# Attention scores from stacked high and low key parts: whole-array matmuls in place of 64-row pairs, in a top-k attention and gated feed-forward kernel

## The chip, the cores and the metric

The kernel runs on one core of one Trainium2 chip. The time is device microseconds of one execution; three runs were taken.

## What is computed

Inputs are q, k and v of 4 batches, 8 heads, 576 positions and 64 dimensions, two feed-forward weights of 512 x 1536 and one of 1536 x 512, and a norm weight. The weights come as 64-bit floats.

```
scores = (q @ k.T) / 8                      # per batch and head, 576 x 576
kth    = 32nd largest of each row
attn   = softmax(where(scores >= kth, scores, -1e9))
x      = (attn @ v), heads side by side     # 2304 x 512
xn     = x / sqrt(mean(x*x) + 1e-6) * rms_g
g      = xn @ w_gate
out    = (g * sigmoid(g) * (xn @ w_val)) @ w_out
```

The scores need more than one reduced-precision pass, since the 32nd largest must be found exactly enough. Each operand is split in a high part (a copy into the reduced type F32R) and a low part (what the copy lost), and the products of the parts are summed in PSUM.

## The kernel before

**Steps and jobs.** The work is cut into 72 steps. An ordinary step is one block of 128 queries for one pair of heads (e = 0 and 1); a tail step takes the last 64 queries of two pairs. A batch has 16 ordinary and 2 tail steps. Two ordinary steps, or one tail step, make a job, which has its own query preparation (`prep_q` and its like, through `turned`). A step makes scores for 576 keys in two halves of 288 for each head, so four PSUM banks: two halves times two heads.

**A step's chain.** `attend` adds the score matmuls (TensorE, PE), four copies of a bank to the SBUF tile `sp` (ScalarE, ACT), then `topk` (VectorE, DVE): elementwise minimum and maximum of the two halves (`mn`, `mx`), then rounds of eight maxima (MAX8) and their removal (MATCH_REPLACE8). Then come the threshold `bt` (GpSimd, POOL), a mask `rr` (ACT), its subtraction (POOL), the exponential with its row sums (ACT), nine transposes of `sp` (PE, L575), their copies, and the value products (PE, `pt`/`ptt` with `vt`).

**Feed-forward.** Ten units of 128 or 256 tokens (`feed_forward`). Each does rows of gate and value matmuls (`wgh`, `wgl`, `wvh`, `wvl` with `xth`, `xtl`; called gate matmuls below, 256 columns) and of output matmuls (`wo`, 512 columns). The gate weights stay in SBUF. The output weights pass through two buffers `wo`, 512 KB a load; the first unit makes them and stores them in `wosc`, later units load them from there. The weights' 64-bit halves are turned to 32-bit floats in 36 pieces of 128 x 512: two VectorE operations each (L357, L358), one of ACT, two of POOL, and again one of ACT for the high part. A raw piece comes into `xvt`, `tg` or later `kraw`.

**Row tiling in the scores.** A head has 64 dimensions, so the two heads of a pair lie on rows 0 to 63 and 64 to 127 of the tiles `kh`, `kl` (keys, high and low) and `qh`, `ql`. For each half there are three products, qh kh, ql kh and qh kl, for each head: twelve matmuls of 64 rows and 288 columns in an ordinary step, alternating between the heads.

**What sets the order.** All operations are recorded in a plan with a priority (`pri`, the step's number plus offsets from the table `PR`), a duration and the keys that they read and write. `place` lays them out engine by engine; `emit` writes every engine's instructions in the order of the starts that `place` finds. Each engine then runs its own list in order. SP's list holds all DMAs, so a DMA that waits there holds back those behind it. Score, transpose, gate and other short-lived results share six banks; two are kept for the output sums.

The program has a second, exact version behind a flag that is not set with these inputs; it is not executed.

Of the kernel before, what the change touches and what calls it, by code (L numbers as in the profile page):

```python
# [9 lines left out]
F32 = mybir.dt.float32  # L10
F32R = mybir.dt.float32r
U32 = mybir.dt.uint32
# [12 lines left out]
    HV=7, SU=1, ZU=6, F1=5.02, FX0=-3.08, FS0=0.39, FD0=-2.4, Z0=0, QN=0, FE=-9.01, EV=-2.13, SO=-2.7, WP1=0.21, WI=-6.69, FO=2.17, FS=0.8, ZP=0, KO=-4.26, WP0=1.0, FB=3.5, AO=0.79, FX=-16.28, QO=-3, TB=0.35, WO=-1.76, SM=1.12,  # L25
# [13 lines left out]
SWITCH = 0.2  # L39

# [191 lines left out]
def tile_topk_attention_moe(  # L232
# [25 lines left out]
    def sb(name, shape, dt=F32):  # L258
        return cp.tile(list(shape), dt, name=name, tag=name)
# [3 lines left out]
    NS, NK, NV, NQ, NPT, NWO, NQR = 5, 4, 2, 3, 4, 2, 2  # L263
# [5 lines left out]
    kh = [sb(f"kh{i}", [128, S + 64], F32R) for i in range(NK)]  # L269
    kl = [sb(f"kl{i}", [128, S + 64], F32R) for i in range(NK)]  # L270
# [3 lines left out]
    qh = [sb(f"qh{i}", [128, 2, 128], F32R) for i in range(NQ)]  # L274
    ql = [sb(f"ql{i}", [128, 2, 128], F32R) for i in range(NQ)]
# [38 lines left out]
    def build(exact):  # L314
# [22 lines left out]
        def weight_piece(src, half, hi, lo, keyh, keyl, pri):  # L337
# [9 lines left out]
            else:  # L347
# [51 lines left out]

        def prep_k(b, pair, pri):  # L400

# [5 lines left out]
            ko = pri + PR["KO"]  # L407
            if g == 0:
# [17 lines left out]
            add(PE, 0.44, tr, r=(("kraw", g, 0), ("kraw", g, 1)), w=(("kh", s, 0), ("kl", s, 0), ("pt", z)), bank=bank, pri=ko)  # L426
            split(bank, z, 512, kh[s][:, 64:576], kl[s][:, 64:576], ("kh", s, 0), ("kl", s, 0), ko)
# [17 lines left out]
        def turned(raw, rkeys, pri):  # L445
# [8 lines left out]
            add(PE, 0.218, tr, r=rkeys, w=(("qh", s), ("ql", s), ("pt", y)), bank=bank, pri=pri + PR["QO"])  # L454
            hi, lo = (t[s].rearrange("p z t -> p (z t)") for t in (qh, ql))
            split(bank, y, 256, hi, lo, ("qh", s), ("ql", s), pri + PR["QO"])
# [35 lines left out]
        def topk(i, e, bank, pri):  # L492
# [18 lines left out]
            add(DVE, 0.372, lambda: nc.vector.tensor_tensor(mn[:, e, :], bank.tile[:, 0:half], b, op=ALU.min), r=bk, w=(nk,), bank=bank, pri=pri)  # L511
            add(DVE, 0.37, lambda: nc.vector.tensor_tensor(row[:, 0:half], bank.tile[:, 0:half], b, op=ALU.max), r=bk + (("turn", 0),), w=(mk,), bank=bank, pri=pri)
# [380 lines left out]
```

## Time and profile before

| | |
|---|---|
| median of 3 runs | 878.14 us (877.94 to 878.2) |
| profiled execution, its own time | 879.04 us |
| its span, first to last instruction | 876.8 us |
| TensorE busy | 798.7 us, 91% |
| VectorE busy | 726.7 us, 83% |
| ScalarE busy | 617.6 us, 70% |
| GpSimd busy | 488.1 us, 56% |
| mean granted TensorE clock | 0.95 |

The profiled execution takes 2.2 us more than its span. Busy time is a share of the whole span; stages differ. PE's rows give each matmul from its start to its modelled end, and matmuls overlap, so the distance between the starts of two rows says what one costs. A line number of a helper (L321) stands for many matmuls; the tile names tell them apart.

### The profile page before, as it was taken

Reading aid. Unit: us, or ns where it says so; the run is one execution under the profiler, and the core shown is the slowest. Engines: PE = TensorE matmul, PEld = TensorE weight load, DVE = VectorE, ACT = ScalarE, POOL = GpSimd, SP = SyncE. Lnnn points to the kernel's source line nnn. Section 1 sums busy time; section 2 is a strip of 40 time slices with the busy share of each in tenths; the row PEclk is TensorE's granted clock in tenths of the full one; section 3 lists DMA queues with packets and bytes.
Section 4 is the critical chain, followed back from the end, with each engine's and each line's share of the span. In section 5 each row is a group of like instructions: output and inputs, shape, how many; then the busy total and the mean of one; then the engine's idle time right before and its main releaser. Section 6 shows DMA issues by size and latency. Waiting matters only on the chain.

```text
span 876.8 us, 19543 instructions
## 1 busy us (share of the span) xinstructions
PE 798.7 (91%) x6770; PEld 701.6 (80%) x6770; DVE 726.7 (83%) x2292; ACT 617.6 (70%) x1529; POOL 488.1 (56%) x690
## 2 busy tenths in 40 slices
PE   5656766899799999999999999999999999999996
PEld 3545745788598888989988888999889988889995
DVE  5999989999889999999899999659998469993211
ACT  6777775898687888778777887666786557874221
POOL 5778989866644564457553644665654244444121
PEclk9978766799799999999999999999999999999998
DMA  7443676455633333244343332333532252232353
GB/s 209 127 117 117 225 224 219 151 172 156 198 96 93 100 108 102 90 111 142 101 145 101 118 120 93 107 121 110 179 93 67 83 174 85 91 127 95 112 164 107
DMA packets 86653, 112.92 MB, mean 129 GB/s; under 512 B 50832, under 2 KB 64144, under 8 KB 86544
## 3 DMA queue, kind: packets, MB, share of 16 engines
q1 hardware_dynamic: 86544, 111.57, 40.8%
q8 instruction: 55, 0.90, 0.4%
q14 instruction: 54, 0.44, 0.2%
HBM read 100.53 MB, written 11.01 MB: 127 GB/s over the span
## 4 chain that ended last, share of the span: by engine, by line
PE 77%; DVE 10%; DMA 6%; ACT 3%; POOL 2%; issue 1%; SPq 0%; DVEq 0%; ACTq 0%; POOLq 0%
PE bank L321 66%; PE bank L575 8%; DVE mx L516 2%; DVE mx L518 2%; DMA wo<-wosc 2%; DMA xvt<-in_moe_w_gate_dram 2%; PE bank L425 1%; DVE bank L357 1%; PE bank L453 1%; DMA kraw<-in_k_dram 1%; DMA xvt<-in_moe_w_out_dram 1%; DVE mx L513 1%; ACT sp L552 1%; PE bank L672 1%; PE bank L637 1%
## 5 line engine op out<-in xcount | busy, mean ns | idle before, releaser
L516 DVE MAX8 mx<-mx 128x8 f32<-128x296 f32 x576 | 242.4, 455 | 0.0
L551 POOL TENSOR_TENSOR sp<-sp,rr 128x576 f32<-128x576 f32 x144 | 184.2, 1290 | 44.7 <-ACT rr L550 42.8
L518 DVE MATCH_REPLACE8 mx<-mx 128x296 f32<-128x296 f32 x432 | 192.2, 451 | 0.0
L321 PE MATMUL bank<-wo,hh 128*128 128x512 f32 x432 | 149.4, 426 | 11.8 <-DMA wo<-wosc 8.4
L740 POOL TENSOR_TENSOR hl<-tg,hh 128x256 fp32r<-128x256 f32 x108 | 79.5, 737 | 115.8 <-ACT hh L739 105.7
L575 PE MATMUL bank<-ident,sp 128*128 128x128 f32 x648 | 100.1, 286 | 29.1 <-ACT sp L552 25.5
L552 ACT ACTIVATE sp<-sp,bt 128x576 f32<-128x576 f32 x144 | 113.1, 787 | 13.7 <-POOL sp L551 13.0
L550 ACT ACTIVATE rr<-sp,bt 128x576 bf16<-128x576 f32 x144 | 108.5, 779 | 17.7 <-POOL bt L546 17.4
L539 ACT COPY sp<-bank 128x288 f32<-128x288 f32 x288 | 97.1, 409 | 24.2 <-PE bank L321 23.4
L321 PE MATMUL bank<-xth,wgh 128*128 128x256 f32 x384 | 113.5, 296 | 0.2 <-ACT xv L593 0.2
L575 PEld LDWEIGHTS bank<-ident,sp 128*128 128x128 f32 x648 | 77.6, 146 | 43.8 <-ACT sp L552 30.6
L321 PE MATMUL bank<-xth,wvh 128*128 128x256 f32 x384 | 110.5, 288 | 0.0
L321 PE MATMUL bank<-xth,wgl 128*128 128x256 f32 x384 | 107.2, 279 | 0.0
L321 PE MATMUL bank<-xtl,wgh 128*128 128x256 f32 x384 | 107.2, 279 | 0.0
L321 PE MATMUL bank<-xth,wvl 128*128 128x256 f32 x384 | 107.2, 279 | 0.0
L321 PE MATMUL bank<-xtl,wvh 128*128 128x256 f32 x384 | 107.2, 279 | 0.0
L727 DVE SCALAR_TENSOR_TENSOR tg<-tg,bank 128x256 f32<-128x256 f32 x108 | 44.3, 411 | 68.5 <-ACT tg L721 68.3
L577 ACT COPY pt<-bank 128x512 f32<-128x512 f32 x144 | 83.1, 595 | 13.1 <-PE bank L575 12.6
L321 PEld LDWEIGHTS bank<-wo,hh 128*128 128x128 f32 x432 | 71.9, 194 | 25.0 <-DMA wo<-wosc 8.3
L721 ACT ACTIVATE tg<-bank 128x256 f32<-128x256 f32 x108 | 41.3, 383 | 69.0 <-PE bank L321 55.1
L321 PE MATMUL bank<-wo,hl 128*128 128x512 f32 x216 | 86.6, 401 | 0.0
L546 POOL TENSOR_TENSOR bt<-mx,cst 128x6 f32<-128x6 f32 x72 | 14.4, 200 | 125.3 <-DVE mx L516 124.3
(147 smaller groups left out, 2052.6 us busy)
## 6 DMA issues: line engine op xcount, KB each, us to landing
wo<-wosc SPq DMA_DIRECT2D x108, 512.0 KB, 3.4
vt<-in_v_dram SPq DMA_DIRECT2D x52, 256.0 KB, 3.0
xvt<-in_moe_w_gate_dram SPq DMA_DIRECT2D x12, 512.0 KB, 4.5
wosc<-wo SPq DMA_DIRECT2D x12, 512.0 KB, 3.2
kraw<-in_k_dram SPq DMA_DIRECT2D x32, 128.0 KB, 3.1
kraw<-in_moe_w_val_dram SPq DMA_DIRECT2D x8, 512.0 KB, 4.1
qraw<-in_q_dram SPq DMA_DIRECT2D x56, 64.0 KB, 2.8
out_dram<-osb SPq DMA_DIRECT2D x14, 256.0 KB, 2.3
```

What stands on the lines that cost most here:

```text
L321: nc.tensor.matmul(o, l, r, start=start, stop=stop)
L516: add(DVE, 0.381, lambda o8=o8: nc.vector.max(o8, row[:, 0:half + 8]), w=(mk,), pri=pri + 0.1 * n)
L518: add(DVE, 0.436, lambda o8=o8: nc.vector.match_replace(row[:, 0:half + 8], o8, row[:, 0:half + 8], NEG), w=(mk,), pri=pri + 0.1 * n)
L539: add(ACT, 0.32, lambda b=bank[half, e], c0=c0: nc.scalar.copy(sp[s][:, c0:c0 + 288], b.tile[:, 0:288]), w=(("sp", s, e, half),), bank=ban ...
L550: add(ACT, 0.7, lambda e=e, tl=tl: nc.scalar.activation(rr[e], tl, AF.Relu, bias=bt[t][:, e, 2:3], scale=-BIG), r=(("bt", t),) + spkeys(i, ...
L551: add(POOL, 1.27, lambda e=e, tl=tl: nc.gpsimd.tensor_tensor(tl, tl, rr[e], op=ALU.subtract), r=(("rr", e),), w=spkeys(i, e), pri=pri + PR ...
L552: add(ACT, 0.8, lambda e=e, tl=tl: nc.scalar.activation(tl, tl, AF.Exp, bias=bt[t][:, e, 1:2], scale=SCALE, accum_out=sums(e)[0]), r=(("bt ...
L575: nc.tensor.transpose(bank.tile[:, c * 128:(c + 1) * 128], sp[s][:, c0 + c * 128:c0 + (c + 1) * 128], ident)
L577: add(ACT, 0.228 if n == 1 else 0.507, lambda dst=dst, bank=bank, n=n: nc.scalar.copy(dst[:, 0:n * 128], bank.tile[:, 0:n * 128]), w=(key, ...
L721: add(ACT, 0.325, lambda gb=gb, hs=hs: nc.scalar.activation(th[hs], gb.tile[:, 0:256], AF.Tanh, scale=1.0 if halves[0] else 0.5), w=(("th" ...
L727: add(DVE, 0.365, lambda gb=gb, hs=hs: nc.vector.scalar_tensor_tensor(th[hs], th[hs], 1.0, gb.tile[:, 0:256], op0=ALU.add, op1=ALU.mult), ...
L740: add(POOL, 0.75, lambda hs=hs: nc.gpsimd.tensor_tensor(hl[hs], th[hs], hh[hs].bitcast(F32), op=ALU.subtract), r=(("th", hs), ("hh", hs)), ...
```

## The change

Scores become matmuls over all 128 rows. For each pair there are now two key tiles, `kt[s][0]` and `kt[s][1]`, one for each head: one half of the rows holds the head's high part, the other half its low part. The query tiles `qh` and `ql` are twice as wide: for each head they hold the high (or low) part of that head's queries on both halves of the rows. One matmul of `qh` with `kt` gives qh kh + qh kl, one of `ql` gives ql kh + ql kl, so a half for one head takes two matmuls in place of three, and the product of the two low parts is now included.

[...] The query's high copy is 512 columns wide instead of 256; its low part is subtracted into `pt`.

`attend` adds four score operations a step, each with one bank and two matmuls (four in a tail step), where one operation held all four banks. The table of offsets is replaced as a whole; some offsets have a second part that counts for the first 14 steps (`early`, `E0`). `ZP` goes from 0 to 1: in the units from the seventh on, a third of the gate activations go through ACT and POOL instead of VectorE. Three other branches are added that these values leave unused (`WS` = 0, `PM` = 72, `XT` = 99). Queries have two buffers instead of three.

```diff
 PR = dict(
-    HV=7, SU=1, ZU=6, F1=5.02, FX0=-3.08, FS0=0.39, FD0=-2.4, Z0=0, QN=0, FE=-9.01, EV=-2.13, SO=-2.7, WP1=0.21, WI=-6.69, FO=2.17, FS=0.8, ZP=0, KO=-4.26, WP0=1.0, FB=3.5, AO=0.79, FX=-16.28, QO=-3, TB=0.35, WO=-1.76, SM=1.12,
+    HV=7, SU=1, ZU=6, F1=5.02, FX0=-7.15, FS0=0.7, FD0=-1.96, Z0=0, QN=0, FE=-19.78, EV=-3.28, SO=-3.29,
+    WP1=0.16, WI=-20.3, FO=3.68, FS=1.61, ZP=1, KO=-6.3, WP0=-0.38, FB=2.24, AO=1.66, FX=-38.8, QO=-2.58, TB=0.32,
+    WO=0.93, SM=12.66, PM=72, WS=0, XT=99, E0=14, SME=2.03, AOE=0.77, SOE=4.91, QOE=-1.17, KOE=1.58, NWO=2,
 )
...
+def early(name, i):
+
+    return PR[name] + (PR[name + "E"] if i < PR["E0"] else 0)
...
-    kh = [sb(f"kh{i}", [128, S + 64], F32R) for i in range(NK)]
-    kl = [sb(f"kl{i}", [128, S + 64], F32R) for i in range(NK)]
+    kt = [[sb(f"kt{i}{e}", [128, S + 64 * (1 - e)], F32R) for e in range(2)] for i in range(NK)]
+    klo = [sb(f"klo{i}", [128, S + 64], F32R) for i in range(2)]
...
+        def move(dst, src, r, w, pri):
+            n = src.shape[1]
+            add(SP, 0.62, lambda: nc.sync.dma_start(dst.bitcast(F32), src.bitcast(F32)), r=r, w=w, pri=pri, nbytes=64 * 4 * n)
...
+            move(kt[s][1][lower, :], kt[s][0][upper, 0:S], first, second, ko)
+            move(kt[s][0][upper, 64:], klo[g][lower, 64:], lows, first, ko)
+            move(kt[s][1][upper, :], klo[g][upper, 0:S], lows, (("ks", s, 1, "l"),), ko)
...
-            hi, lo = (t[s].rearrange("p z t -> p (z t)") for t in (qh, ql))
-            split(bank, y, 256, hi, lo, ("qh", s), ("ql", s), pri + PR["QO"])
...
+            add(ACT, 0.51, lambda: nc.scalar.copy(hi, bank.tile[:, 0:256].unsqueeze(1).to_broadcast([128, 2, 256])), w=(("qh", s, 0), ("qh", s, 1)), bank=bank, pri=qo)
+            add(ACT, 0.29, lambda: nc.scalar.copy(tmp, bank.tile[:, 0:256]), w=(tk,), bank=bank, pri=qo)
+            lo = pt[y][:, 256:512].bitcast(F32R)
+            add(POOL, 0.73, lambda: nc.gpsimd.tensor_tensor(lo, tmp, hi[:, 1, :].bitcast(F32), op=ALU.subtract), r=(("qh", s, 1),), w=(tk,), pri=qo)
+
+            lower, upper = slice(0, 64), slice(64, 128)
+            move(hi[upper, 0, :], hi[lower, 0, :], (), (("qh", s, 0),), qo)
+            move(hi[lower, 1, :], hi[upper, 1, :], (), (("qh", s, 1),), qo)
+            for e, src in ((0, lower), (1, upper)):
+                for y2, dst in enumerate((lower, upper)):
+                    move(ql[s][dst, e, :], lo[src, :], (tk,), (("ql", s, e, y2),), qo)
...
-            terms = [(col, pair, qq, kk) for pair, col in cols for qq, kk in ((qh, kh), (ql, kh), (qh, kl))]
-
-            def sm():
-                for half in (1, 0):
-                    for n, (col, pair, qq, kk) in enumerate(terms):
-                        for e in range(2):
-                            es = slice(64 * e, 64 * e + 64)
-                            c0 = 64 * (1 - e) + half * 288
-                            mm(bank[half, e].tile[:, 0:288], qq[qs][es, col, :], kk[pair % NK][es, c0:c0 + 288], n == 0, n == len(terms) - 1)
...
             for half in (1, 0):
                 for e in range(2):
+                    terms = [(col, pair, qq) for pair, col in cols for qq in (qh, ql)]
+
+                    def sm(half=half, e=e, terms=terms):
+                        for n, (col, pair, qq) in enumerate(terms):
+                            mm(bank[half, e].tile[:, 0:288], qq[qs][:, e, col * 128:(col + 1) * 128], kt[pair % NK][e][:, 64 * (1 - e) + half * 288:64 * (1 - e) + half * 288 + 288], n == 0, n == len(terms) - 1)
...
+                    add(PE, 0.25 * len(cols), sm, r=(("qh", qs, e), ("ql", qs, e, 0), ("ql", qs, e, 1)) + kk, w=(("sp", s, e, half),) + ((("turn", e),) if not exact and half == 0 else ()), bank=bank[half, e], pri=so)
```

**PE, the scores of the first step, before.** `kh0`, `kl0` are the first pair's high and low keys, `qh0`, `ql0` its queries; each row is one matmul.

```order
L321 MATMUL bank4_67<-kh0_79,qh0_92 128x288
L321 MATMUL bank5_68<-kh0_79,qh0_92 128x288
L321 MATMUL bank4_67<-kh0_79,ql0_95 128x288
L321 MATMUL bank5_68<-kh0_79,ql0_95 128x288
L321 MATMUL bank4_67<-kl0_83,qh0_92 128x288
L321 MATMUL bank5_68<-kl0_83,qh0_92 128x288
L321 MATMUL bank0_63<-kh0_79,qh0_92 128x288
L321 MATMUL bank1_64<-kh0_79,qh0_92 128x288
L321 MATMUL bank0_63<-kh0_79,ql0_95 128x288
L321 MATMUL bank1_64<-kh0_79,ql0_95 128x288
L321 MATMUL bank0_63<-kl0_83,qh0_92 128x288
L321 MATMUL bank1_64<-kl0_83,qh0_92 128x288
```

The same place now; `kt00` and `kt01` are the stacked keys of the first pair's two heads.

```order
L328 MATMUL bank1_64<-kt00_79,qh0_94 128x288
L328 MATMUL bank1_64<-kt00_79,ql0_96 128x288
L328 MATMUL bank4_67<-kt00_79,qh0_94 128x288
L328 MATMUL bank4_67<-kt00_79,ql0_96 128x288
L328 MATMUL bank5_68<-kt01_80,qh0_94 128x288
L328 MATMUL bank5_68<-kt01_80,ql0_96 128x288
L328 MATMUL bank0_63<-kt01_80,qh0_94 128x288
L328 MATMUL bank0_63<-kt01_80,ql0_96 128x288
```

Twelve matmuls that alternated between two banks are eight that finish one bank after the other.

**VectorE, the start of the program, before.** TENSOR_SCALAR and SCALAR_TENSOR_TENSOR with `xvt` or `tg` are one weight piece; `mn` and `mx` with `sp0` begin the first step's top-k.

```order
L420 TENSOR_TENSOR kl0_83<-bank1_64,kh0_79 128x2x64
L420 TENSOR_TENSOR kl1_84<-bank1_64,kh1_80 128x2x64
L357 TENSOR_SCALAR bank3_66<-xvt_125 128x512
L358 SCALAR_TENSOR_TENSOR x0_122<-xvt_125,bank3_66 128x512
L357 TENSOR_SCALAR bank2_65<-tg_128 128x512
L358 SCALAR_TENSOR_TENSOR osb_133<-tg_128,bank2_65 128x512
L511 TENSOR_TENSOR mn_106<-bank0_63,sp0_98 128x288
L512 TENSOR_TENSOR mx_105<-bank0_63,sp0_98 128x288
```

Now:

```order
L368 TENSOR_SCALAR bank0_63<-xvt_125 128x512
L369 SCALAR_TENSOR_TENSOR x0_122<-xvt_125,bank0_63 128x512
L436 TENSOR_TENSOR klo0_87<-bank3_66,kt00_79 128x2x64
L368 TENSOR_SCALAR bank4_67<-tg_128 128x512
L369 SCALAR_TENSOR_TENSOR osb_133<-tg_128,bank4_67 128x512
L436 TENSOR_TENSOR klo1_88<-bank3_66,kt10_81 128x2x64
L368 TENSOR_SCALAR bank0_63<-xvt_125 128x512
L369 SCALAR_TENSOR_TENSOR qrt_93<-xvt_125,bank0_63 128x512
L368 TENSOR_SCALAR bank2_65<-tg_128 128x512
L369 SCALAR_TENSOR_TENSOR x0_122<-tg_128,bank2_65 128x512
L368 TENSOR_SCALAR bank3_66<-xvt_125 128x512
L548 TENSOR_TENSOR mn_106<-bank4_67,sp0_98 128x288
```

Two weight pieces stood ahead of the first minimum; now four and the first half of a fifth do.

**SP, the same start, now** (before, the list begins with two `kraw`, two `krawt`, `qraw0`, `xvt` and `tg`, and the next `xvt` is its fifteenth DMA). Rows from `kt`, `klo`, `qh` or `pt` are the moves.

```order
L331 DMA xvt_125<-in_moe_w_gate_dram 128x1024
L331 DMA kraw_77<-in_k_dram 128x4x64 x2
...
L331 DMA xvt_125<-in_moe_w_gate_dram 128x1024
L331 DMA krawt_78<-in_k_dram 64x2x64
L413 DMA kt01_80<-kt00_79 64x576
L413 DMA qh0_94<-qh0_94 64x256
L413 DMA ql0_96<-pt2_118 64x256 x2
L331 DMA tg_128<-in_moe_w_val_dram 128x1024
L413 DMA kt01_80<-klo0_87 64x576
L413 DMA kt00_79<-klo0_87 64x576
L331 DMA xvt_125<-in_moe_w_gate_dram 128x1024
```

The first weight load moved ahead of the keys, and the moves of the first job stand between the second and the third load of `xvt`.

## Rows read from the trace of the kernel before

**Rows 1.** The page's first part: busy time in us, share of the span, instructions.

```profile
PE 798.7 (91%) x6770; PEld 701.6 (80%) x6770; DVE 726.7 (83%) x2292; ACT 617.6 (70%) x1529; POOL 488.1 (56%) x690
```

**Rows 2.** Four stretches of the span: start and end, length, then busy us and instructions of PE, PEld (weight loads), DVE, ACT and POOL, then PE's granted clock, the DMA share and GB/s.

```profile
0.00:160.00 160.00, 101.92 (x632) 80.01 (x632) 143.28 (x398) 114.25 (x261) 130.92 (x159) 0.80 0.58 180
...
207.00:240.00 33.00, 25.34 (x204) 20.16 (x203) 28.01 (x91) 24.13 (x61) 22.14 (x36) 0.84 0.56 173
240.00:560.00 320.00, 318.06 (x2916) 282.71 (x2914) 305.63 (x1012) 254.91 (x650) 170.49 (x253) 1.00 0.36 107
560.00:877.00 317.00, 306.88 (x2612) 277.33 (x2611) 205.04 (x647) 181.84 (x453) 133.93 (x207) 0.99 0.36 116
```

**Rows 3.** The chain that ended last, by engine (the page's fourth part).

```profile
PE 77%; DVE 10%; DMA 6%; ACT 3%; POOL 2%; issue 1%; SPq 0%; DVEq 0%; ACTq 0%; POOLq 0%
```

**Rows 4.** The longest of PE's waits from 207 to 240 us: in total, times, longest.

```profile
PE bank L321 <- DMA wo<-wosc: 5.9, 3, 3.5
```

**Rows 5.** VectorE's timeline where the maxima of step 15 and of step 25 begin: start, duration.

```profile
193.96 0.81 DVE L512 TENSOR_TENSOR mx<-bank,sp 128x288 f32<-128x288 f32 x2
...
293.15 0.45 DVE L512 TENSOR_TENSOR mx<-bank,sp 128x288 f32<-128x288 f32 x1
```

**Rows 6.** PE's timeline: the first transposes of steps 15, 16, 17 and 25, most of a value product, a score step (400.42 on) and the edge of a wo group (804.41 on).

```profile
206.91 0.60 PE L575 MATMUL bank<-ident,sp 128*128 128x128 f32 x4
...
210.82 1.04 PE L321 MATMUL bank<-pt,vt 128*64 128x128 f32 x16
...
235.11 0.60 PE L575 MATMUL bank<-ident,sp 128*128 128x128 f32 x4
...
239.78 0.44 PE L575 MATMUL bank<-ident,sp 128*128 128x128 f32 x2
...
309.14 0.71 PE L575 MATMUL bank<-ident,sp 128*128 128x128 f32 x5
...
400.09 0.40 PE L321 MATMUL bank<-wo,hl 128*128 128x512 f32 x1
400.42 0.40 PE L321 MATMUL bank<-kh,qh 64*128 64x288 f32 x2
400.66 0.29 PE L321 MATMUL bank<-kh,ql 64*128 64x288 f32 x2
...
401.18 0.30 PE L321 MATMUL bank<-kl,qh 64*128 64x288 f32 x2
401.41 0.38 PE L321 MATMUL bank<-xth,wgh 128*128 128x256 f32 x1
401.63 0.28 PE L321 MATMUL bank<-xtl,wgh 128*128 128x256 f32 x1
...
402.10 0.29 PE L321 MATMUL bank<-xth,wgl 128*128 128x256 f32 x1
...
804.41 0.63 PE L321 MATMUL bank<-wo,hh 128*128 128x512 f32 x2
805.12 0.28 PE L321 MATMUL bank<-xth,wgh 128*128 128x256 f32 x1
```

**Rows 7.** The weight loads (PEld) of whole-array gate matmuls.

```profile
401.51 0.19 PEld L321 LDWEIGHTS bank<-xtl,wgh 128*128 128x128 f32 x1
401.63 0.19 PEld L321 LDWEIGHTS bank<-xth,wgl 128*128 128x128 f32 x1
```

**Rows 8.** A piece of the chain in order of time: nine transposes, start and us.

```profile
249.28 0.98 PE bank L575 x9
```

**Rows 9.** The timeline of the start, with SP's DMA issues.

```profile
3.47 0.60 SPq L324 DMA_DIRECT2D qraw<-in_q_dram  x1
4.11 0.50 SPq L324 DMA_DIRECT2D xvt<-in_moe_w_gate_dram  x1
8.08 0.69 DVE L357 TENSOR_SCALAR bank<-xvt 128x512 uint32<-128x512 uint32 x1 [0.58 <-DMA xvt<-in_moe_w_gate_dram]
8.81 0.69 DVE L358 SCALAR_TENSOR_TENSOR x<-xvt,bank 128x512 uint32<-128x512 uint32 x1
12.57 0.45 DVE L512 TENSOR_TENSOR mx<-bank,sp 128x288 f32<-128x288 f32 x1
```

**Rows 10.** The page's DMA issues: how many, KB each, median us to landing.

```profile
wo<-wosc SPq DMA_DIRECT2D x108, 512.0 KB, 3.4
kraw<-in_k_dram SPq DMA_DIRECT2D x32, 128.0 KB, 3.1
qrt<-in_q_dram SPq DMA_DIRECT2D x16, 32.0 KB, 2.2
```

**Rows 11.** Two of ScalarE's groups: busy us, mean ns, idle before.

```profile
L396 ACT CAST qh<-bank 128x256 fp32r<-128x256 f32 x40 | 15.3, 382 | 2.8 <-PE bank L453 1.4
L397 ACT COPY pt<-bank 128x512 f32<-128x512 f32 x16 | 9.5, 595 | 0.0
```

**Rows 12.** VectorE's two longest waits from 200 to 260 us.

```profile
DVE mn L511 <- ACT sp L539: 3.2, 1, 3.2
DVE rs L555 <- ACT sp L552: 2.3, 1, 2.3
```

**Rows 13.** VectorE's two longest waits from 20 to 200 us.

```profile
DVE mn L511 <- ACT sp L539: 1.9, 2, 1.7
DVE ss L657 <- ACT bank L651: 1.5, 1, 1.5
```

More of the change, by code (lines that the diff above doesn't have):

```diff
@@ L425, in tr @@
                     nc.tensor.transpose(bank.tile[:, c * 128:(c + 1) * 128], kraw[:, g, c].rearrange("p h d -> p (h d)"), ident)
-            add(PE, 0.44, tr, r=(("kraw", g, 0), ("kraw", g, 1)), w=(("kh", s, 0), ("kl", s, 0), ("pt", z)), bank=bank, pri=ko)
-            split(bank, z, 512, kh[s][:, 64:576], kl[s][:, 64:576], ("kh", s, 0), ("kl", s, 0), ko)
+            add(PE, 0.44, tr, r=(("kraw", g, 0), ("kraw", g, 1)), w=tuple(("ks", s, e, n) for e in range(2) for n in "ml") + (("klo", g, 0), ("pt", z)), bank=bank, pri=ko)
+            split(bank, z, 512, kt[s][0][:, 64:576], klo[g][:, 64:576], ("ks", s, 0, "m"), ("klo", g, 0), ko)
+            lower, upper = slice(0, 64), slice(64, 128)
+            first, second = (tuple(("ks", s, e, n) for n in "mt") for e in range(2))
+            lows = (("klo", g, 0), ("klo", g, 1))
+            move(kt[s][1][lower, :], kt[s][0][upper, 0:S], first, second, ko)
+            move(kt[s][0][upper, 64:], klo[g][lower, 64:], lows, first, ko)
+            move(kt[s][1][upper, :], klo[g][upper, 0:S], lows, (("ks", s, 1, "l"),), ko)
         vcount = [0]
@@ L510, in topk @@
             b, bk = sp[s][:, e * S + half:(e + 1) * S], (("sp", s, e, 1),)
[L511 to L512 removed]
+            if i >= PR["PM"]:
+                add(POOL, 0.73, lambda: nc.gpsimd.tensor_tensor(mn[:, e, :], sp[s][:, e * S:e * S + half], b, op=ALU.min), r=spk, w=(nk,), pri=pri)
+            else:
+                add(DVE, 0.372, lambda: nc.vector.tensor_tensor(mn[:, e, :], bank.tile[:, 0:half], b, op=ALU.min), r=bk, w=(nk,), bank=bank, pri=pri)
+            add(DVE, 0.37, lambda: nc.vector.tensor_tensor(row[:, 0:half], bank.tile[:, 0:half], b, op=ALU.max), r=bk + (("turn", e),), w=(mk,), bank=bank, pri=pri)
             add(DVE, 0.371, lambda: nc.vector.max(row[:, half:half + 8], mn[:, e, :]), r=(nk,), w=(mk,), pri=pri)
@@ L554, in invert @@
+                add(ACT, 0.8, lambda e=e, tl=tl: nc.scalar.activation(tl, tl, AF.Exp, bias=bt[t][:, e, 1:2], scale=SCALE, accum_out=sums(e)[0]), r=(("bt", t),), w=spkeys(i, e) + (sums(e)[1],), pri=pri + early("SM", i))
         def invert(rslot, sl, keys, key, pri):
@@ L808, in build @@
                 )
-                attend_out_tail(i, b, p, vs, rslot, i + PR["AO"])
+                attend_out_tail(i, b, p, vs, rslot, i + early("AO", i))
                 if b == B - 1 and p == 1:
```

64 lines of the change are left out of this document (37 added, 27 removed).

## The prediction

> **What bounds the kernel now.** I read the page's shares first [rows 1], then four stretches of the span [rows 2], then the chain [rows 3]. TensorE (PE) is busy 91% of the span and VectorE 83%; the chain is 77% PE and 10% VectorE. The stretches say when each of them counts. Up to 160 us VectorE works 143 of 160 us and PE only 102, at a granted clock of 0.80 of full: VectorE makes the top-32 and unpacks weights, and PE has little that is ready. From 240 to 560 PE is busy 318 of 320 us at clock 1.00, and VectorE 306. From 560 on VectorE falls to 205 of 317 and PE carries the end alone. So the end comes at the time when PE is saturated plus the work that is then still behind it. The stretch 207 to 240 is the last one in which PE loses much: 25 of 33 us busy, clock 0.84, and it waits 5.9 us for wo loads [rows 2, 4].
>
> Two points show how the engines hang together. Step 15's maxima start on VectorE at 193.96, its transposes on PE at 206.91 [rows 5, 6]: 12.95 us, the shortest such distance that I found from step 6 on, so there PE waits for VectorE (top-k, then softmax). Step 25's maxima start at 293.15 and its transposes at 309.14 [rows 5, 6]: 16.0 us, so there VectorE has some 3.1 us to spare. Both are near being the bound there.
>
> **What one score step costs on PE.** In [rows 6] the twelve 64-row matmuls run as six pairs; from 400.66 to 401.18 they stand 0.13 us apart, 0.131 on average. Four edges come on top. Three wo matmuls take 0.71 us elsewhere there (804.41 to 805.12), 0.235 each; the one ahead of the group takes 0.33 (400.09 to 400.42): +0.09. The first pair takes 0.24 (to 400.66): +0.11. The last takes 0.23 (401.18 to 401.41): +0.10. The first gate matmul behind takes 0.22 (to 401.63) where the next four take 0.117 each (to 402.10): +0.10. So each entry or exit of the row tiling costs 0.20 us, and a step 6 x 0.131 + 0.40 = 1.19 us. Whole-array matmuls of 256 columns stand 0.117 us apart, so 288 columns take 0.131 us, no faster than a pair. The new step has eight: 1.05 us without edges. A tail step goes from 12 pairs, 1.97 us, to 16 matmuls, 2.10 us. Over the program the order counts 480 pairs before and 640 matmuls now (+20.9 us), and 272 edges of row or column tiling before, 144 now (-25.6): **-4.7 us** of PE work.
>
> Do the new weight loads stay hidden? Whole-array loads of the gate matmuls take 0.19 us each and start 0.12 us apart, under the matmuls [rows 7]. Such cover hides 640 score loads too; without it they would add 640 x 0.19 = 122 us. The Trainium skill, "TensorE: Matmul & The Clock Gate", Part 3, section The mechanism, says that a weight load overlaps a running matmul only when their row groups differ, which would speak for the old pairs and against this change. The loads of [rows 7], all of one row group, contradict it here, and the sum goes by that view.
>
> **Step by step through the order.** I count what stands behind a place and price it by [rows 6, 8]: 0.117 a gate matmul, 0.235 a wo matmul, 0.131 a pair or a new score matmul, 0.109 a transpose, 0.20 an edge. Behind step 17's transposes (239.78 [rows 6]) stand, before and now: gate matmuls 2304 and 2256 (-5.6), 348 pairs against 454 score matmuls (+13.9), edges 201 and 110 (-18.2), all else equal: **-9.9**.
>
> Between step 15's and step 17's transposes PE had 18 gate and 24 wo matmuls, 24 pairs, 51 transposes, two value products of some 1.2 us (1.04 the longer part of one, at 210.82) and 9 edges: 20.6 us of work in 32.9. It was held by the wo loads: 24 wo matmuls took 206.91 to 235.11, 1.17 us each. In the new order 90 gate, 27 wo and 42 score matmuls, 54 transposes, the same products and 4 edges lie there: 31 us of work beside 27 x 1.17 = 31.7 us of wo chain. Work now fills the waits. I take 31.7 plus 2.8 for imperfect cover: 34.5, **+1.6** (-1.2 with perfect cover, +10.6 if the old loss of 12.3 comes on top of the work).
>
> **The start.** VectorE now does four and a half weight pieces before its first minimum instead of two, and the third xvt piece can only be loaded when the second is unpacked. In [rows 9] a piece costs 0.69 + 0.73 us, and an xvt load is unpacked 3.97 us after its issue (4.11 to 8.08). With xvt first on SP: landed at 4.7, unpacked at 6.2, second load issued at 6.6, landed at 10.7, unpacked at 12.2; the third stands on SP behind eighteen DMAs, six of them moves, at about 0.6 us each [rows 9], is issued at 12.8, landed at 16.9, and the first maximum follows at about 18.1. Before it was 12.57 [rows 9]. Of these 5.5 us 3.6 are pieces done early: **+2** (0 if they come faster, +5 if the moves wait for their sources and hold the load). Up to step 15 VectorE's work is otherwise equal in both orders (15 steps, all 36 pieces).
>
> **The moves.** 48 for keys and 240 for queries, 288 more DMAs on SP. No transfer within SBUF is in the trace; the nearest rows take 2.2 us (32 KB) to 3.1 us (128 KB) [rows 10], and 0.6 us of SP each [rows 9]. SP's own time grows by 288 x 0.6 = 173 us, 20% of the span; it only counts where a load stands behind it (below). A query's moves go out a job ahead, two steps of about 10 us (99 us from step 15 to 25 [rows 5]), hidden; without that lead, some 3.5 us a job. Where the batch changes, the new keys pass copy, subtraction and move with two top-k steps (20 us) of lead, and the last key move of the pair stands on SP behind a wo load. I take **+1** (0 to +5: one transfer with its issue at one or two changes). The query copy is 512 wide instead of 256: 0.595 for 0.382 us [rows 11], 40 x 0.21 = 8.5 us on ScalarE, which is busy 70%: nothing (8.5 if it were the bound). The third of the last units' gates that goes to ScalarE and GpSimd relieves VectorE where it is idle: nothing.
>
> **Sum.** -9.9 + 1.6 + 2 + 1 = -5.3 by PE. VectorE has a say: behind step 25's transposes stand 12 gate matmuls more (1.4), 402 matmuls for 300 pairs (+13.4), 78 edges fewer (-15.6): -0.8. Less the 3.1 spare there, plus 2 for the start: -1.9. By that reading most of PE's lead at step 17 would be lost waiting for VectorE. But VectorE itself waited 5.5 us at two places between 200 and 260 [rows 12], for score copies and row sums that hang on PE while PE stood at the wo loads; I take them as won with those waits: -7.4. The later of the two, -5.3, holds. The profiled execution took 879.04 us, 2.2 outside its span of 876.8, and stands 0.9 above the median 878.14: 873.7 profiled, **873 us** against the median.
>
> **Rivals.**
> VectorE does not win its waits back: -1.9, and 1 for the moves: 877 us, no change to be told. For it: both engines are within 3 us of each other at step 25, and two balanced engines wait for each other. Against: the waits of [rows 12] hang on PE.
> VectorE sheds its waits before 200 us too, 3.4 us in the two longest [rows 13], as score ops of one bank no longer need four at once, and the wo chain is wholly covered (2.8): 873 - 6.2 = 867 us. Against it: only 1.9 are for score copies.
> SP blocks (the other side). A feed-forward row of 24 gate and 6 wo matmuls takes 4.2 us; a wo load 3.4 [rows 10], 0.5 to issue, 1.4 in use: two buffers leave about 3 us. Six query moves are 3.7 us of issue, more if one waits for GpSimd. If each of 40 such groups costs 0.4 us beyond that slack, 16 us: 889 us; from 0.13 us each the gain is gone. Against it: the moves stand in pieces, with wo loads between.
> Exposed loads: if each new score matmul waits for its own load, 873 + 122 = 995 us; [rows 7] speak against it. This is what the rule quoted above would do.
>
> **Chances.** The sum (868 to 876 as its own range) 0.45, waits kept 0.16, waits shed 0.18, SP blocks 0.20, exposed loads 0.01. A measurement of this kernel tells 0.2% (1.8 us) from no change. Faster 0.64 (0.43 of the sum, 0.18, 0.03 of waits kept), same 0.14 (0.02 and 0.12), slower 0.22 (0.01, 0.20, 0.01). The range 860 to 888 leaves out the tails of shed waits and of a blocked SP.
>
> **What would show it.** Right: score matmuls 0.13 us apart, no edges beside them; VectorE's first maximum near 18 us; PE's waits for wo between 207 and 240 down to 2 or 3 us; step 17's transposes near 243 us with PE saturated from there. Wrong: idle PE waiting for softmax between 240 and 330 us, wo waits that grow after 240, or score matmuls more than 0.14 us apart.

## The result, and the profile after

The changed kernel takes 891.31 us (median of 4 runs, 888.88 to 892.53) against 878.17 (4 runs of the kernel before beside it): ratio 1.0136, 95% interval 1.011 to 1.0162. It is slower by 1.4%, clear of no change, where 873 us and a range of 860 to 888 had been forecast. Its profiled execution took 892.53 us, with a span of 890.7. "Transfers" below are the 288 DMAs that `move` adds, from one place in SBUF to another: 48 for keys (144 KB each) and 240 for queries (64 KB each).

Part 1 of the page of the changed kernel, to be held against [rows 1], and its chain, against [rows 3]:

```profile
PE 799.8 (90%) x6450; PEld 717.5 (81%) x6450; DVE 723.4 (81%) x2276; ACT 628.7 (71%) x1545; POOL 512.8 (58%) x722
...
PE 67%; DMA 13%; DVE 11%; ACT 3%; POOL 2%; issue 2%; SPq 1%; DVEq 0%; POOLq 0%; ACTq 0%
```

The two engines that bound the kernel, TensorE and VectorE, have no more work than before. What grew is the share of the chain that is a transfer: 13% for 6%. Three of the stretches of [rows 2] (start, end, length, busy us of PE, PEld, DVE, ACT, POOL, granted clock, DMA share, GB/s):

```profile
0.00:160.00 160.00, 96.84 (x552) 76.49 (x552) 136.19 (x391) 113.68 (x257) 118.83 (x139) 0.82 0.63 182
207.00:240.00 33.00, 27.95 (x207) 24.32 (x204) 24.42 (x80) 22.50 (x60) 20.65 (x34) 0.90 0.78 220
240.00:560.00 320.00, 314.00 (x2746) 287.31 (x2745) 306.67 (x1009) 257.54 (x647) 169.33 (x248) 1.00 0.49 141
```

VectorE did 136.2 us of work in the first 160 where it did 143.3 before: it is 7 us behind when the first stage ends, and that stage is its own. In the stretch around the batch change it has 24.4 us for 28.0.

The score step on PE, at 398.5 us (start, duration), and a weight load under it:

```profile
398.47 0.38 PE L328 MATMUL bank<-kt,qh 128*128 128x288 f32 x1
398.69 0.29 PE L328 MATMUL bank<-kt,ql 128*128 128x288 f32 x1
398.82 0.30 PE L328 MATMUL bank<-kt,qh 128*128 128x288 f32 x1
```

```profile
398.82 0.19 PEld L328 LDWEIGHTS bank<-kt,ql 128*128 128x128 f32 x1
```

The second and the third stand 0.13 us apart (the 0.22 before them is at the edge to transposes), and a 0.19 us load lies under the third, as forecast. What the new data path waits for is another matter. The three sorts of PE's waits in the whole span that name the transfers or the loads of wo (in total, times, longest):

```profile
PE bank L328 <- DMA ql<-pt: 20.8, 10, 7.4
...
PE bank L328 <- DMA kt<-klo: 6.5, 3, 4.5
...
PE bank L328 <- DMA wo<-wosc: 4.0, 7, 1.3
```

27 us of waits for transfers within SBUF. PE's waits for softmax fell from 25.5 to 10.9 us in the same span, so part of the new waits stands where PE waited before, and this is no price yet. The page's DMA issues give them 2.1 to 2.9 us from issue to landing:

```profile
ql<-pt SPq DMA_DIRECT2D x160, 64.0 KB, 2.1
...
kt<-klo SPq DMA_DIRECT2D x32, 144.0 KB, 2.9
```

Two places show how they come into the path. The start, first on SP and then on VectorE, against [rows 9]:

```profile
8.31 0.60 SPq L413 DMA_DIRECT2D kt<-kt  x1
8.96 0.59 SPq L413 DMA_DIRECT2D qh<-qh  x1
9.65 1.18 SPq L413 DMA_DIRECT2D ql<-pt  x2
10.95 0.52 SPq L331 DMA_DIRECT2D tg<-in_moe_w_val_dram  x1
11.56 1.90 SPq L413 DMA_DIRECT2D kt<-klo  x2
13.95 0.33 SPq L331 DMA_DIRECT2D xvt<-in_moe_w_gate_dram  x1
```

```profile
16.63 0.70 DVE L368 TENSOR_SCALAR bank<-tg 128x512 uint32<-128x512 uint32 x1 [2.75 <-DMA tg<-in_moe_w_val_dram]
...
20.34 0.70 DVE L368 TENSOR_SCALAR bank<-xvt 128x512 uint32<-128x512 uint32 x1 [2.22 <-DMA xvt<-in_moe_w_gate_dram]
...
21.31 0.45 DVE L549 TENSOR_TENSOR mx<-bank,sp 128x288 f32<-128x288 f32 x1
```

Six transfers stand ahead of the weight load of 13.95, and the first maximum comes at 21.31 for 12.57 before. VectorE idles 2.75 and 2.22 us for weights whose loads SP had already issued: they are unpacked 5.7 and 6.4 us after their issues at 10.95 and 13.95, where [rows 9] had 4.0. The wait is for slow landings; the kernel without the transfers, below, says how much the place on SP adds. The batch change, PE, then SP, then the chain:

```profile
232.66 0.37 PE L328 MATMUL bank<-kt,qh 128*128 128x288 f32 x1 [1.20 <-DMA qh<-qh]
235.41 0.58 PE L328 MATMUL bank<-kt,ql 128*128 128x288 f32 x1 [2.38 <-DMA ql<-pt]
```

```profile
226.55 0.60 SPq L413 DMA_DIRECT2D qh<-qh  x1
...
228.52 1.69 SPq L413 DMA_DIRECT2D ql<-pt  x2
```

```profile
224.25 5.48 DMA wo<-wosc
...
229.75 5.53 DMA ql<-pt
```

GpSimd had made the low parts of these queries by 227.0. PE at 235.41 waits for the second of the two transfers from 228.52 on. By the chain it was issued at 229.75, when a wo load of 224.25 had landed, and then took 5.5 us itself; the page's medians are 2.1 us for such a transfer and 3.7 for a wo load. The transfer of the high part, issued at 226.55, let PE go 6.1 us later. So PE loses 3.6 us here (1.20 and 2.38) to an issue that waits for another load and, more, to slow landings, in a stretch in which the DMA engines move 220 GB/s for 173 before (busy share 0.78 for 0.56). That the traffic makes them slow is argued here, not shown. Adding up SP's issue rows, its queue was taken 24 of the first 40 us before and 31 now, and from 208 to 250 us 20 of 42 before and 30 now. The marks that the prediction set, in PE's and VectorE's timelines (steps 15, 17 and 25; before in [rows 5, 6]):

```profile
212.89 0.60 PE L609 MATMUL bank<-ident,sp 128*128 128x128 f32 x4
...
253.16 0.60 PE L609 MATMUL bank<-ident,sp 128*128 128x128 f32 x4
...
314.64 0.60 PE L609 MATMUL bank<-ident,sp 128*128 128x128 f32 x4
```

```profile
199.39 0.81 DVE L549 TENSOR_TENSOR mx<-bank,sp 128x288 f32<-128x288 f32 x2
...
301.37 0.81 DVE L549 TENSOR_TENSOR mx<-bank,sp 128x288 f32<-128x288 f32 x2
```

Late by 5.4 us at step 15's maxima, 13.4 at step 17's transposes (forecast 3.6), 5.5 at step 25's, and 13.9 at the end. So 8.4 of the 13.9 us come behind step 25, where the prediction had 0.8 less work.

### The profile page after: what moved, and what is told of

Its sections match the earlier page's. It is cut to its first block, busy times and chain, and to the rows that moved or that the text cites. A ratio compares the mean times of both kernels' runs of the same rounds, so it can differ in the third digit from the quotient of the medians.

```text
span 890.7 us, 19628 instructions
## 1 busy us (share of the span) xinstructions
PE 799.8 (90%) x6450; PEld 717.5 (81%) x6450; DVE 723.4 (81%) x2276; ACT 628.7 (71%) x1545; POOL 512.8 (58%) x722
## 4 chain that ended last, share of the span: by engine, by line
PE 67%; DMA 13%; DVE 11%; ACT 3%; POOL 2%; issue 2%; SPq 1%; DVEq 0%; POOLq 0%; ACTq 0%
PE bank L328 57%; PE bank L609 7%; DMA wo<-wosc 4%; DMA ql<-pt 3%; DVE mx L553 3%; DVE mx L555 3%; DVE bank L368 1%; DMA kt<-klo 1%; DMA vt<-in_v_dram 1%; PE bank L476 1%; DMA xvt<-in_moe_w_out_dram 1%; DVE mx L550 1%; DMA kt<-kt 1%; PE bank L671 1%; DMA tg<-in_moe_w_val_dram 1%
## 5 line engine op out<-in xcount | busy, mean ns | idle before, releaser
L328 PE MATMUL bank<-wo,hh 128*128 128x512 f32 x432 | 144.8, 415 | 9.0 <-DMA wo<-wosc 4.0
L573 ACT COPY sp<-bank 128x288 f32<-128x288 f32 x288 | 105.9, 408 | 36.3 <-PE bank L328 34.2
L328 PE MATMUL bank<-kt,qh 128*128 128x288 f32 x320 | 103.7, 336 | 22.0 <-DMA ql<-pt 7.4
L609 PE MATMUL bank<-ident,sp 128*128 128x128 f32 x648 | 102.6, 288 | 15.2 <-ACT sp L586 10.9
L328 PE MATMUL bank<-xth,wgh 128*128 128x256 f32 x384 | 111.3, 290 | 0.0
L328 PE MATMUL bank<-kt,ql 128*128 128x288 f32 x320 | 96.4, 315 | 13.6 <-DMA ql<-pt 13.5
L609 PEld LDWEIGHTS bank<-ident,sp 128*128 128x128 f32 x648 | 79.8, 147 | 28.4 <-ACT sp L586 15.0
L611 ACT COPY pt<-bank 128x512 f32<-128x512 f32 x144 | 83.9, 593 | 15.6 <-PE bank L609 14.5
L328 PEld LDWEIGHTS bank<-kt,qh 128*128 128x128 f32 x320 | 64.3, 201 | 32.7 <-issue 12.1
```

Of the source, the lines that this page charges most:

```text
L328: nc.tensor.matmul(o, l, r, start=start, stop=stop)
L573: add(ACT, 0.32, lambda b=bank[half, e], c0=c0: nc.scalar.copy(sp[s][:, c0:c0 + 288], b.tile[:, 0:288]), w=(("sp", s, e, half),), bank=ban ...
L609: nc.tensor.transpose(bank.tile[:, c * 128:(c + 1) * 128], sp[s][:, c0 + c * 128:c0 + (c + 1) * 128], ident)
L611: add(ACT, 0.228 if n == 1 else 0.507, lambda dst=dst, bank=bank, n=n: nc.scalar.copy(dst[:, 0:n * 128], bank.tile[:, 0:n * 128]), w=(key, ...
```

## The experiments

Two theories at first. M: the 288 transfers cost the time. O: the new order and its retuned table cost it, by the late start and by a VectorE that is the bound up to step 25.

**Without the transfers.**

```
-            add(SP, 0.62, lambda: nc.sync.dma_start(dst.bitcast(F32), src.bitcast(F32)), ...)
+            add(SP, 0.62, lambda: None, ...)
```

> The changed kernel in its own order on every engine, but none of the 288 transfers within SBUF is issued. Both halves read the first key tile, and GpSimd writes the queries' low parts straight into the tile that is read, so part of the scores is not the reference's. Theory M (the transfers cost the time: their 0.6 us each on SP and their 2.1 to 2.9 us to landing): the third xvt load is issued some 6 us earlier, VectorE's first maximum comes at 15 to 17 us instead of 21.3, TensorE's waits for these transfers (some 12 us up to 40 us, 17 us behind) go, and the time falls to 876 to 882 us. Theory O (the order that goes with the change costs the time, by more weight pieces ahead of the first top-32 and by a VectorE that is the bound up to step 25): the first maximum stays near 20 us and the time stays at 887 to 892 us.

871.65 us (5 runs, 870.04 to 876.43), ratio to before 0.9917 (0.9889 to 0.9944). That is below both ranges that were expected, so M holds by more than it said: with the very same order on the other engines the transfers cost 891.3 - 871.7 = 19.7 us (by the two ratios to before 19.2, give or take 3.3), and the rest of the change gives 6.5. Its start, on SP and on VectorE:

```profile
11.35 0.33 SPq L331 DMA_DIRECT2D tg<-in_moe_w_val_dram  x1
13.32 0.33 SPq L331 DMA_DIRECT2D xvt<-in_moe_w_gate_dram  x1
```

```profile
14.89 0.69 DVE L368 TENSOR_SCALAR bank<-tg 128x512 uint32<-128x512 uint32 x1 [1.64 <-DMA tg<-in_moe_w_val_dram]
...
17.44 0.69 DVE L368 TENSOR_SCALAR bank<-xvt 128x512 uint32<-128x512 uint32 x1 [1.06 <-DMA xvt<-in_moe_w_gate_dram]
...
18.41 0.45 DVE L549 TENSOR_TENSOR mx<-bank,sp 128x288 f32<-128x288 f32 x1
```

18.4, not the 15 to 17 that M expected: two thirds of the late start (5.8 of 8.7 us) are the order's. Nor is the third xvt load issued some 6 us earlier, as M had it, but 0.6 (13.32 for 13.95), and the tg load ahead of it is 0.4 later. What differs is the landing: the two are unpacked 3.5 and 4.1 us after their issue, beside the transfers 5.7 and 6.4. So most of the 2.9 us that the transfers cost at the first maximum are slower landings of the weights, and little is their place on SP. The profiled execution was the slowest of its five (876.43, span 874.5), so its trace shows the gain some 5 us short. Its transposes of steps 15, 17 and 25 on PE:

```profile
206.47 0.60 PE L609 MATMUL bank<-ident,sp 128*128 128x128 f32 x4
...
242.44 0.60 PE L609 MATMUL bank<-ident,sp 128*128 128x128 f32 x4
...
302.76 0.60 PE L609 MATMUL bank<-ident,sp 128*128 128x128 f32 x4
```

**The transfers aside, then small, then with sources that never wait.** Three kernels in the same order take the 19.7 us apart.

```
+    away = dp.tile([32, 64, S], F32, ...)           # scratch in HBM, region by turns
-    nc.sync.dma_start(dst, src)
+    nc.sync.dma_start(away[turn, :, 0:n], src)      # aside
+    nc.sync.dma_start(away[turn, :, 0:2], src[:, 0:2])   # small
+    (query transfers take a tile written once at the start)   # unheld
```

> As the kernel without the transfers, but all 288 are issued at their places with their sources and sizes, into a scratch in HBM that nobody reads: SP's time and the traffic are back, the waits for landing are not. If the landings that TensorE waits for are what the transfers cost, the time is within 2 us of the kernel without transfers; if SP's queue or the traffic is what they cost, it is within 3 us of the changed kernel (891 us). Theory O expects both near 890 us.

> As the kernel whose transfers go aside into a scratch in HBM (885.4 us, against 871.7 without transfers), but each carries two elements a partition instead of 256 or 576; sources, places and number are kept, part of the scores is again not the reference's. If the traffic costs the 13.7 us: 872 to 876 us. If the issues on SP cost them (their own time or their waiting for sources): 883 to 888 us.

> As the kernel whose transfers go aside, in full size, but the 240 of the queries take a tile that is written once at the start, so SP never waits for ScalarE or GpSimd ahead of them; part of the scores is again not the reference's. If waiting for sources is what holds SP's queue: 873 to 878 us. If the issue time or the traffic is: 883 to 888 us.

Aside 885.37 us (883.7 to 889.08, 6 runs), small 882.05 (881.17 to 884.63, 10 runs), unheld 885.21 (883.06 to 888.31, 6 runs). So of 19.7 us, 10.4 come with the issues and almost no bytes (871.65 to 882.05), some 3.3 with the bytes, and 5.9 with transfers that land where they are read (885.4 to 891.3). In the 5.9 three things are not told apart: the landings that PE waits for, SBUF instead of HBM as the place written, and the missing dependence on the low key parts. Waiting for the queries' sources costs nothing that shows (885.21 for 885.37). The 3.3 are uncertain, the ratios of the two kernels to before (1.0049, 1.0028 to 1.007, and 1.0083, 1.0053 to 1.0113) overlap. Neither branch expected of the first kernel fits: landings alone make less than a third of the price, and issues and traffic not all of it. The second kernel is a us below the branch of the issues, the third within its branch. Step 15's maxima show the same order, without transfers, with small ones, and with full ones aside (199.39 in the changed kernel):

```profile
190.66 0.45 DVE L549 TENSOR_TENSOR mx<-bank,sp 128x288 f32<-128x288 f32 x1
```

```profile
193.58 0.80 DVE L557 TENSOR_TENSOR mx<-bank,sp 128x288 f32<-128x288 f32 x2
```

```profile
195.71 0.45 DVE L557 TENSOR_TENSOR mx<-bank,sp 128x288 f32<-128x288 f32 x1
```

Where transfers go aside, PE's waits from 160 to 255 us are for wo again, 5.4 us; without transfers these are 3.1.

**Early or late ones.** The 102 transfers that belong to the steps up to the batch change left out, the 186 others aside.

```
+    (lambda: nc.sync.dma_start(spare(n), src)) if pri > 20 else (lambda: None)
```

> As the kernel whose transfers go aside, but the 102 transfers that belong to the steps up to the batch change at step 18 to 20 are not issued, the 186 behind it are; part of the scores is not the reference's. If the issues cost by where they stand, at the start and at the batch change, where SP's queue is 73 to 85% taken: within 4 us of the kernel without transfers, 872 to 876 us. If they cost by number: 871.7 + 13.7 x 186/288 = 880.5 us.

877.51 us (872.15 to 881.04, 8 runs), between the two expectations: the late 186 cost 5.9 us, 0.03 each, the early 102 cost 885.4 - 877.5 = 7.9, 0.08 each. By the ratios to before it is 4.8 and 9.7, each give or take some 3.7, so an early one costs more, but how much more is uncertain. Its step 25 on PE, 14.5 us ahead of the changed kernel's 314.64, which is the whole of its lead at the end (spans 875.9 and 890.7):

```profile
300.11 0.49 PE L617 MATMUL bank<-ident,sp 128*128 128x128 f32 x3
```

**The same transfers on the kernel before.** Its own order on four engines, the 288 added on SP as soon as GpSimd has made a low part.

```
+                for part in (hi, lo, lo, hi, lo, lo) if n == 256 else (hi, lo, lo):
+                    nc.sync.dma_start(away[turn, :, 0:n], part[h:h + 64].bitcast(F32))
```

> The kernel before, in its own order on TensorE, VectorE, ScalarE and GpSimd, with 288 transfers more on SP (for each set of queries six of 64 KB, for each key pair three of 128 KB, issued when GpSimd has made the low part) into a scratch in HBM that nobody reads. If 288 issues and their traffic cost a kernel with this work 10 to 14 us wherever they stand: 888 to 893 us. If the loss belongs to the changed order, and the old one has slack on SP: 878 to 881 us.

919.07 us (918.84 to 923.28), ratio 1.047 (1.0431 to 1.0509): 41 us, three times what was expected and three times the 13.7 of the transfers aside in the changed order. Each stands on SP right behind its source here, and SP waits 10.0 us for GpSimd's low query parts ahead of them, for 1.7 in the changed kernel. So an order that is not planned around them pays more; how much is SP's waiting was not taken apart. PE's waits for wo from 210 to 260 us, beside the 5.9 of [rows 4]:

```profile
PE bank L324 <- DMA wo<-wosc: 17.4, 6, 4.9
```

**Other places on SP.** The transfers up to 3 us of planned time earlier, or up to 1.3 us later, everything else in its order.

```
+            if getattr(o, "early", 0):
+                start[i] = max([start[i] - o.early] + [start[p] + 1e-6 for p, _ in o.pred])
+            if getattr(o, "late", 0):
+                start[i] = max(start[i], min([start[i] + o.late] + [start[s] - 1e-6 for s, _ in o.succ]))
```

> A correct kernel in the changed one's order, in which each of the 288 transfers stands on SP up to 3 us of planned time earlier, as far as its source allows, ahead of loads that the planner had put before it. If TensorE's waits for landings can be had back by this: 885 to 888 us. If the loads that now stand behind them are as urgent: 890 to 896 us.

> A correct kernel in the changed one's order, with each transfer up to 1.3 us of planned time later on SP, so that loads stand ahead of it, as far as the score op that reads it allows. If the loads behind the transfers are what is held: 884 to 889 us. If the landings that TensorE waits for grow by as much: 892 us or more.

911.61 us earlier (910.02 to 913.58) and 936.96 later (931.92 to 941.46). Both directions lose, 20 and 46 us, the first far more than either branch expected. PE's waits say what grew: earlier, those for loads that now stand behind; later, those for the landings. The first fence is the kernel with the transfers earlier, the second that with them later (PE's waits, whole span):

```profile
PE bank L331 <- DMA ql<-pt: 19.0, 17, 2.9
...
PE bank L331 <- DMA wo<-wosc: 8.9, 10, 2.2
```

```profile
PE bank L331 <- DMA ql<-pt: 43.4, 30, 6.0
PE bank L331 <- DMA kt<-klo: 19.0, 4, 9.7
```

The waits for wo went from 4.0 to 8.9 us in the one, those for query transfers from 20.8 to 43.4 in the other. The 4.9 us that wo loads cost more are a quarter of the first loss; the rest of it was not taken apart. Shifted all together, the transfers have no slack; single ones were not tried.

**Another queue.**

```
-    nc.sync.dma_start(dst, src)
+    nc.scalar.dma_start(dst, src)     # in the other kernel nc.gpsimd
```

> A correct kernel in the changed one's order; the 288 transfers within SBUF are issued by ScalarE's queue instead of SP's, at the same place in time. If SP's issue time is what costs 10 us and ScalarE (busy 71%) has room: SP's loads go out earlier, 878 to 883 us. If ScalarE then holds its copies and exponentials behind the issues (0.6 us each, 173 us in all, would bring it to 90%): 892 us or more.

> The same with GpSimd's queue (busy 58%), which makes the low parts that most of the transfers carry. If an issue there costs no more than on SP: 878 to 883 us. If it holds the subtractions that softmax waits for: 892 us or more.

926.45 us (924.31 to 927.75) and 992.54 us (988.9 to 994.93), far worse. ScalarE's timeline:

```profile
302.45 2.80 ACTq L413 DMA_DIRECT2D ql<-pt  x2
305.30 0.78 ACT L586 ACTIVATE sp<-sp,bt 128x576 f32<-128x576 f32 x1 [2.71 <-DMA ql<-pt]
```

An exponential stands 2.7 us behind two issues: here issues, with what they wait for, hold work that softmax needs, which on SP they don't. GpSimd's largest group of issues (busy us, mean ns, idle before):

```profile
L413 POOL DMA_DIRECT2D ql<-pt x160 | 85.3, 535 | 3.6 <-POOL pt L483 2.2 <-issue 0.2 <-POOL bt L580 0.2
```

GpSimd's busy time rose from 512.8 to 662.7 us. The Trainium skill, DMA: Bandwidth & Descriptors, section Rules for kernel authors, says that spreading transfers over the engines' queues does not help bandwidth and only saves issue time. No run here measures that bandwidth. The runs show that the issue time is paid where it goes: 0.54 us each on GpSimd.

**Fewer transfers.** High and low query parts in one tile, one transfer for three, 128 in all; first in the changed order, then ordered anew.

```
+    qs2 = [sb(f"qs{i}", [128, 2, 2, 256], F32R) for i in range(NQ)]
+    nc.gpsimd.tensor_tensor(ql[s], tmp.unsqueeze(1).to_broadcast([128, 2, 256]), hi, op=ALU.subtract)
+    for e, src, dst in ((0, lower, upper), (1, upper, lower)):
+        move(qs2[s][dst, e], qs2[s][src, e], ...)
```

> A correct kernel in the order of the changed one with fewer transfers: high and low query parts lie in one tile, GpSimd writes the low parts 512 wide (0.54 us more, 40 times), and one transfer of both parts takes the place of three, 128 in all instead of 288. If the number of issues counts: 19.7 x 128/288 = 8.8 us above the kernel without transfers, 880 us. If waiting for sources or landings counts, which are all still there: 886 to 892 us.

> The same fewer transfers, with the planner told of them, so that it orders the work anew. By the number of issues about 880 us, give or take 5 for another order; if sources and landings count, 886 us or more. Under 876 it would beat both kernels.

888.79 us (886.11 to 894.4), ratio 1.011 (1.0063 to 1.0157), not told apart from the changed kernel, and 912.6 (909.01 to 913.19) with a new order. At 10.4 us for 288 issues, 160 fewer should have given 5.8; 2.5 came, and that is not told from nothing. The high part now goes out only with the low part, which GpSimd makes later, so PE's waits for query transfers hardly fell; where the saved issue time went is not shown, and it is a reason not to read the 10.4 as a price for each issue. PE's waits of the first of the two (in the changed kernel 20.8 for ql<-pt):

```profile
PE bank L328 <- DMA qs<-qs: 19.0, 10, 4.9
```

**The table.** All knobs back at their old numbers, then only the two that place the first weight pieces.

```
-    WP1=0.16, ... WP0=-0.38,
+    WP1=0.21, ... WP0=1.0,
```

> The changed kernel's data path with the numbers of the kernel before in the planner's table (the knobs that are new stand at nothing, no unit's gate goes to ScalarE and GpSimd). Theory O: the start is that of before (first maximum near 15 us, step 15's maxima near 196 us) and the time falls to 876 to 883 us. Theory M: the 288 transfers are all there, so the time stays at 889 us or more, whatever the numbers.

> The changed kernel with two numbers of the table back at their old values, those that place the first eight weight pieces: two pieces instead of four and a half stand ahead of the first top-32. If the late start is what the kernel carries to its end: first maximum near 15 us, step 15's maxima near 195.5 us instead of 199.4, and 886 to 888 us. If the pieces are only done later in the place of the first steps (VectorE has the same work up to step 15): step 15's maxima within 1.5 us of 199.4, and 889 to 893 us.

901.84 us (898.94 to 905.04) and 905.57 us (903.48 to 907.72). Theory O falls: the retuned table is worth 10 us, the pieces ahead of the first top-32 are no loss. The second kernel fits neither branch expected of it: its start was earlier (18.8 for 21.3), but its step 15's maxima came at 208.4 and the time was 14 us longer. VectorE's work up to 208 us shows where it fell behind. The third busy number of each row is VectorE's; the changed kernel and the one with the weight pieces later:

```profile
0.00:208.00 208.00, 139.27 (x898) 113.88 (x899) 182.34 (x528) 152.67 (x350) 158.67 (x193) 0.85 0.64 190
```

```profile
0.00:208.00 208.00, 132.28 (x856) 109.88 (x856) 174.67 (x498) 146.96 (x335) 155.00 (x188) 0.84 0.63 182
```

182.3 and 174.7 us (185.0 without transfers). VectorE's waits for the xvt and tg loads, 9.9 us there and 11.7 in the changed kernel, do not explain it. Why one order keeps VectorE fed and another doesn't was not taken further apart. No kernel that does the whole computation was faster than the one before.

## Why the prediction was wrong

The step that failed is the one on the moves: "A query's moves go out a job ahead ... hidden ... I take +1 (0 to +5)". They cost 19.7: 10.4 with the issues, some 3.3 with the bytes and 5.9 with landings where they are read. It priced a late landing at one or two places and said of SP's 173 us that they only count "where a load stands behind it", but put a price on that only in a rival. In the stages that decide, loads do stand behind it, and the profile of before had both halves of that: VectorE was the bound up to 160 us and lived on weight loads from SP, and the batch change already waited for wo loads. The step should have asked how full SP's queue was there (24 of 40 us and 20 of 42, from its issue rows) and what 0.6 us more, several times in a row, would delay. It also took the landing times of the old kernel: 2.2 to 3.1 us for a transfer and 4.0 for a weight load, where the places that decide had 5.5 to 6.1 and 5.7 to 6.4.

Put 19.7 in the place of 1 and the sum gives 892; the measured time was 891.3. That is closer than its parts, and so luck in part:

- **The score step**: right. Matmuls 0.13 us apart, loads hidden, no edges beside them. Without transfers PE went from step 17's transposes to step 25's in 60.3 us, for 69.4 before; the count of matmuls and edges had said 9.1 less, but 7.0 of that are 60 gate matmuls that the new order does later. The edges are tried behind step 25: the count had said -0.8 and the rows give +4.0 (571.7 for 567.7). Adding up the distances of PE's rows beyond those usual for their neighbours, some 3 us of it are waits, most for wo. So the counted prices, the edges' 0.20 us among them, hold within some 2 us there.
- **From step 15 to step 17**: forecast 34.5 us. Without transfers 36.0, with them 40.3. The wo waits went, as said; those for qh<-qh and ql<-pt at 232 and 235 us took their place, through landings of 5.5 and 6.1 us that the sum did not have.
- **The start**: forecast 18.1 for the first maximum, 18.4 without transfers, 21.3 with them. The upper end of +5 ("if the moves wait for their sources and hold the load") is near the 5.4 by which step 15 came late, but its mechanism is not what happened: the third xvt load left SP at 13.95, forecast 12.8, and took 6.4 us to be unpacked, where the sum had 4.1 to its landing. Without transfers step 15's maxima were 3.3 us ahead of before and its transposes 0.4, where +2 was forecast: the pieces done early were fully won back.
- **VectorE's waits**: "I take them as won" is not borne out. In the stretch of [rows 12] VectorE waited 6.0 us for score copies without transfers and 7.6 with them; with the late ones alone it was 2.8, so single executions differ. The way from step 25's maxima to its transposes shrank from 16.0 to 13.3 us: VectorE's spare there is gone, and it shares the bound, as the rival that keeps these waits had it.
- **The rival "SP blocks"** (889 us, 0.20) came nearest: issues with almost no bytes brought 10.4 of the 19.7 us. That its time lies 2 us from the measured one is luck in part. Its 40 groups of 0.4 us behind wo loads are shown by no run, and slow landings of weights at the start and of transfers at the batch change, which it did not have, belong to the rest.
- Of the three signs "Wrong" in the prediction one came true, in small: PE's waits for wo after 240 us grew from 2.6 to 4.0. None named a wait for the new transfers.

Not settled: how the 10.4 us of the issues divide between VectorE's weights and PE's wo loads, why 160 fewer issues gave so little, what makes landings slow at the batch change, and why the orders from other tables differ by 10 to 20 us. Not tried: a third buffer for queries, as before the change, and any other way than DMAs to bring the parts to the other rows.

## What to carry to other kernels

A transfer that is "issued a job ahead" is not free: price its issue on the queue that it joins, stage by stage, against the loads behind it, and its landing where the lead is shortest. Where an engine lives on loads from that queue, count the queue as an engine: its busy time per stretch, before and with the additions. Do not take a landing time from a quieter stretch or kernel: loads and transfers that cross land later, and the loads that were there before pay too. And look at how much of a counted gain is the change and how much is work that a new order puts elsewhere.

## What had not been expected of the hardware

- An issue of a transfer within SBUF takes 0.46 to 0.6 us on SP, about 0.5 on ScalarE and 0.54 on GpSimd, whatever queue it stands in; that of a transfer of 2 elements a partition cost the kernel nearly as much as the full one (882.05 and 885.4 us for 288 of them, 871.65 without).
- 64 KB within SBUF take 2.1 us from issue to landing, 144 KB 2.9 (medians): not less than 128 KB from HBM (3.1 before, [rows 10]) by much. At the batch change 64 KB took 5.5 and 6.1 us.
- SP's issue rows carry eight semaphores in turn, so an issue can also wait for a landing that has nothing to do with it: SP's waits name wo, xvt and vt loads ahead of transfers within SBUF (2.4, 2.1 and 0.9 us in the whole span). The chain at 229.75 us is such a case: the semaphore of that transfer was last that of the wo load of 224.25. This was only read, not tried.
- Transfers slow their neighbours: wo loads land in 3.7 us, 3.6 beside the small transfers, and 3.4 in the same order without any; two weight loads of the start took 5.7 and 6.4 us for 3.5 and 4.1.
